# Hashed attention with an expert layer behind it: the six transposes of an attention step in three pairs, with score products between the pairs

## The chip, the cores and the metric

The kernel runs on one core of a Trainium2 chip. The metric is the device time of one execution in microseconds; the time shown for a kernel is the median of several executions. The names of the engines are those of the profile: PE multiplies matrices (PEld is its loading of weights), DVE works on vectors, ACT evaluates activations, POOL is the general engine, and SP issues most of the transfers.

## The reference, cut to what matters

```python
# q, k, v: (4, 8, 768, 64), proj: (64, 6)
q_bits = (np.einsum('bhsd,dk->bhsk', q, proj) > 0)      # 6 signs make a bucket
k_bits = (np.einsum('bhsd,dk->bhsk', k, proj) > 0)
mask = q_bucket[:, :, :, None] == k_bucket[:, :, None, :]
scores = np.where(mask, scale * np.matmul(q, k.transpose(0, 1, 3, 2)), -1000000000.0)
attn = np.exp(scores - np.max(scores, axis=-1, keepdims=True))
attn = attn / (np.sum(attn, axis=-1, keepdims=True) + 1e-09)
out = np.matmul(attn, v)                                # then 3072 tokens x 512
h = x @ w_in                                            # 512 -> 2048
g = h * np.clip(h + 3.0, 0.0, 6.0) / 6.0
result = g @ w_out                                      # 2048 -> 512
```

There are 32 pairs of batch and head, called heads below, with 768 queries and 768 keys each.

## The kernel before, in words

**Tiling.** Attention goes in steps `k` of 128 queries, six steps to a head (`KT = 6`), 192 steps in all. A step has four parts. `scores` (L374) makes the 128 x 768 scores with four matmuls of 384 columns: two on line 387 (`q1` with the two halves of `k1`, 76 rows) and two on line 389 (`q2` with the two halves of `k2`, 128 rows), which add the low parts of the split numbers to the same two banks of PSUM. `lowest` (L391) has DVE copy the scores to a tile `p` and find the row's extreme at once (line 396). `exponential` (L402) has ACT take the exponential in place in `p` (line 408). `transp` (L415) transposes the six 128 x 128 blocks of `p` on PE (line 418), three into each of two banks `pt`; `split_p` (L451) has ACT copy each bank rounded (line 475) and DVE subtract to get the remainder (line 479), and `values` (L491) multiplies both with the values, six matmuls of 256 columns per step on line 501, since a pair of steps shares one bank `acc`. The pair's result is copied out by ACT on line 551.

**Buffers.** Tiles `p` come from two buffers, so that `lowest(k + 2)` writes where the transposes of step `k` read. The scores alternate between two pairs of banks (`pair`). The banks `pt` and `acc`, and the small results `rt` and `h`, come from `bank`, which alternates between two tags of two buffers each: every request gets the bank of the request four before it. Where a pair of steps makes only its own five requests, the order is `pt, pt, acc` in an even step and `pt, pt` in an odd one. So the second bank of an odd step is the one that held the first bank of the even step before it, which DVE's line 479 reads last, and the second bank of an even step is the `acc` of the pair before.

**Order.** PE, DVE, ACT and POOL work in the order in which the program writes their instructions (`manual_schedule`). The loop over `k` (L1224) does, in a step: the transposes of `k`, `exponential(k + 1)`, `lowest(k + 2)`, half of an earlier pair's values, `split_p(k)`, and then `lead(k + 3)`, which calls `scores(k + 3)`. So PE sees, from one step to the next, values of `k`, scores of `k + 3`, transposes of `k + 1`. One step in each head also has the six matmuls of `hash_qk` (lines 334 to 336, tile `z`) ahead of its scores, and DVE's `bits` (line 352) behind them. From `k = 96` on `lead` comes right behind the values in some steps. `normalise` (line 591, tile `rt`) adds two small transposes in some steps.

**Stages.** Steps 0 to 51 run as attention alone, up to about 133 us. Then the expert layer of the first batch runs alone (`first_ffn`). Steps 52 to 100 run as attention alone again, from 277 to about 394 us. From step 101 on `beside_ffn` runs attention beside the expert layer of the other batches; there only step 101 still uses `transp`. The rest of the span is the expert layer.

Of the kernel before, what the change touches and what calls it, by code (L numbers as in the profile page):

```python
# [18 lines left out]
P = 128  # L19
# [9 lines left out]
LA = 3  # L29
# [14 lines left out]
def lsh_attention_moe(  # L44
# [10 lines left out]
    nc = tc.nc  # L55
# [3 lines left out]
    KT = S // P  # L59
    HW = S // 2  # L60
    QT = HW // P
# [5 lines left out]
    KM = D + 2 * NB  # L67
# [25 lines left out]
    def bank(shape, name: str, tag: str | None = None):  # L93

        nonlocal turn
        if tag is None:
            tag = ("pt", "pu")[turn % 2]
            turn += 1
        return ps.tile(shape, F32, name=name, tag=tag, bufs=2)
# [4 lines left out]
    def pair(name: str):  # L104

        nonlocal pair_turn
        pair_turn += 1
        tag = "s" if ffn_on or pair_turn % 2 else "po"
        return ps.tile([P, 2, 512], F32, name=name, tag=tag, bufs=1)
# [5 lines left out]
    ident = cp.tile([P, P], F32, name="ident")  # L115
# [119 lines left out]
    def get_qk(i: int, tag: str = "raw"):  # L235
        b, h = divmod(i, H)
        if tag == "raw":
            raws[i] = sp.tile([P, S], F32, name=f"raw{i}", tag=tag, bufs=1)[:]
        else:
            raws[i] = wide_tile([P, 2 * WC], F32, f"raw{i}")[:, :S]  # L240
        if paced:
            dma(out=raws[i][:D], in_=qkT[b, h, :D])
        else:
            dma(out=raws[i], in_=qkT[b, h])

    def get_k_rows(i: int):
        b, h = divmod(i, H)
        moves.append(lambda: dma(out=raws[i][D:], in_=qkT[b, h, D:]))
# [114 lines left out]
    def split_v(i: int):  # L363
        o = (i % 2) * D
        vr = vrs.pop(i)
        vv = vvs[i] = sp.tile([P, KT, P], F32R, name=f"vv{i}", tag="vv")
        nc.gpsimd.tensor_copy(vv[:, :, o : o + D], vr[:])
        nc.gpsimd.tensor_sub(
            vv[:, :, D - o : 2 * D - o], vr[:], vv[:, :, o : o + D].bitcast(F32)
        )  # L370

    scs, probs, outs = {}, {}, {}

    def scores(g: int):  # L374
        i, t = divmod(g, KT)
        k1, k2, q1, q2 = state[i]
        us = slice(t * P, (t + 1) * P)
        s = scs[g] = pair(f"s{g}")
        def half(x, c: int):
            if g < GT:  # L380
                return x[:, c * HW : (c + 1) * HW]

            x = x.rearrange("p (x g b) -> p g x b", x=KT, g=4)
            return x[:, 2 * c : 2 * c + 2]

        for c in range(2):
            nc.tensor.matmul(s[:, c, :HW], lhsT=q1[:KM, us], rhs=half(k1[:KM], c), start=True, stop=False)  # L387
        for c in range(2):
            nc.tensor.matmul(s[:, c, :HW], lhsT=q2[:, us], rhs=half(k2, c), start=False, stop=True)  # L389

    def lowest(g: int):  # L391

# [19 lines left out]
    pts, parts = {}, {}  # L412
    halves = 0

    def transp(g: int, c: int):  # L415
        pt = pts[g, c] = bank([P, QT, P], f"pt{g}_{c}")
        for x in range(QT):
            nc.tensor.transpose(pt[:, x], probs[g][0][:, c, x * P : (x + 1) * P], ident[:])  # L418
        if c:
            del probs[g]  # L420

# [100 lines left out]
    def add():  # L524
        for _, _, to, of in adds:
            nc.gpsimd.dma_start(out=to, in_=of, accum_op=ALU.add)
        adds[:] = fresh
        fresh.clear()
# [515 lines left out]
        finish()()  # L1044


    def lead(j: int):

        i, t = divmod(j, KT)
        n = i + 1  # L1050
        alone = j <= GF + LA
        if t == 0 and n < NJ:
            split_qk(n, nc.scalar.copy if ffn_on else nc.gpsimd.tensor_copy)
        if t in (1, 4) and not paced:
            add()
        if t == (4 if paced else 2):
            if i:
                split_v(i)
        if t == (3 if paced else 2):

            if n + 1 < NJ and n != H + 1:
                get_qk(n + 1)
                if paced:
                    get_k_rows(n + 1)
        if t == (5 if paced else 3) and n < NJ:
            get_v(n)
        hashed = t == 3 and n < NJ and alone and j != GB - 1
        if hashed:
            hash_qk(n)
        scores(j)  # L1070
        if hashed:
            bits(n)
        if t == (5 if paced else 4) and n + 1 < NJ:
            scale_q(n + 1)
# [27 lines left out]
    def value_half():  # L1102
        nonlocal vnext
        u, c = divmod(vnext, 2)
        vnext += 1
        values(u, c)
        return c == 1
# [14 lines left out]
    with tc.manual_schedule(engines={ET.PE, ET.DVE, ET.Activation, ET.Pool}):  # L1122
# [15 lines left out]
        def beside_ffn(k: int):  # L1138

            nonlocal paced, stage, held
            held = False
            if k < GT:
                for c in range(2):
                    transp(k, c)
                exponential(k + 1)
            for _ in range(2):
                u = vnext // 2
                if u < NS // 2 and (2 * u < GT or k % 2 and k >= 2 * u + 3):  # L1150
                    if vnext % 2 == 0 and k >= GT:
                        value_whole()
                        through.append(u)
                        break
                    if value_half():
                        through.append(vnext // 2 - 1)
                if k < GT:
                    break
            behind = (k - 1 + LA) % KT == 4 or k == GT + 1
            if GT <= k < NS - 2 and not behind:  # L1160
                lowest(k + 2)
            go("A")
            if GT <= k < NS - 2 and behind:
                lowest(k + 2)
            while late_bits:
                bits(late_bits.pop())
            if k < GT:
                for c in range(2):
                    split_p(k, c, False)
                split_lows()  # L1170
                while through:
                    output(through.pop(0))
                flip(k + 1)
            if k + 2 < NS:
                if k < GT:
                    lowest(k + 2)
                    assert len(side) <= 2
                    opening.pop()()
                if k == GT:
                    go("B")  # L1180
                    go("C")
                exponential(k + 2)
            paced = True
            multiply()
            if k + 2 < NS:
                flip(k + 2)
            split = GT <= k - LT < NS
            go("B")
            while rest:
                rest.pop()()  # L1190
            if split:
                split_p(k - LT, 1, False)
            if k == NS + LT:
                homes.clear()
            while through and (through[0] < vnext // 2 - 1 or k % 2 == 0 or k < GT):
                output(through.pop(0))
            hashed = k + LA < NS and (k + LA) % KT == 4 and (k + LA) // KT + 1 < NJ
            if hashed:
                hash_qk((k + LA) // KT + 1)
            if split:  # L1200
                amid.append(lambda: (split_p(k - LT, 0, False), split_lows()))
            go("C")
            while amid:
                amid.pop()()
            split_lows()
            if hashed and k == GT + 1:
                late_bits.append((k + LA) // KT + 1)
            elif hashed:
                bits((k + LA) // KT + 1)
            if k + LA < NS:  # L1210
                lead(k + LA)
            if moves:
                moves.pop(0)()
            if GT <= k + 1 < NS:
                move(k + 1)

            place_in_chunk = (k - GT) % NFC
            if subs and (k % 2 and (k < GT or place_in_chunk != NFC - 1) or k > GT and place_in_chunk == 0):
                subs.pop(0)()
            go("D")  # L1220
            if k % KT in (1, 3):
                add()

        for k in range(NS + LT + 2):  # L1224
# [10 lines left out]
                load_first_x()  # L1235
            if k == HK:
                late["x"] = sp.tile([P, S], F32, name="late", tag="raw", bufs=1)
            for c in range(2):
                transp(k, c)
            if k + 1 < end:  # L1240
                exponential(k + 1)
            if k + 2 < end:
# [19 lines left out]
            hashed = k >= GF and (k + LA) % KT == 2  # L1262
            after = hashed or k >= GF and (k + LA) % KT == 3
            if k >= GF and k + LA < end and not after:
                lead(k + LA)
            for c in range(2):
                split_p(k, c, third)
            split_lows()
# [2 lines left out]
            if (k < GF or after) and k + LA < end:  # L1271
                if hashed:
                    if (k + LA) // KT + 1 < NJ:
                        hash_qk((k + LA) // KT + 1)
                        bits((k + LA) // KT + 1)
                    next(fill, None)
                lead(k + LA)
            if k == GB - 2:
                hash_qk((GB - 1) // KT + 1)
                bits((GB - 1) // KT + 1)  # L1280
# [78 lines left out]
```

## Time and profile before

| what | value |
|---|---|
| time before, median of 3 runs | 965.38 us (964.78 to 966.62) |
| the profiled execution's own time | 964.74 us |
| its span | 963.0 us |
| PE busy | 945.1 us, 98% of the span |
| DVE, ACT, POOL busy | 723.0, 623.5 and 474.2 us |
| transposes of line 418 | 612 (102 steps of six) |
| score matmuls of lines 387 and 389 | 384 each |

The span is the time from the first to the last instruction that the profile shows; what lies around it is the 1.7 us between 963.0 and 964.74. The page's groups give busy time, the mean of one instruction and the idle time that the engine spent just ahead of it, with the engine and line that ended it. The timeline merges neighbouring instructions of one line into one row, and "x6" is their number. A matmul's duration in these rows is the time until its result is there; the next one can start much sooner, so the distance from start to start tells what PE pays for it.

### The profile page before, as it was taken

To read this page: it belongs to the slowest core of one execution; us is meant where nothing else is said; L and a number is where in the kernel's file an instruction comes from. 1 tells how busy PE (TensorE), PEld (TensorE's weight loads), DVE (VectorE), ACT (ScalarE), POOL (GpSimd) and SP (SyncE) were. 2 spreads that over 40 slices of the span, in tenths; PEclk is the share of its full clock that TensorE was granted. 3 is DMA by queue.
4 is the path that set the end of the run, shared out by engine and by line. 5 is a ranking of instruction groups with operands and counts; after the bars stand their busy time and mean duration, and the time that the engine had idled before them with its cause. 6 is when DMAs were issued, how large, how long until landed. Compare 5 with 4: busy or idle time off the path is not lost.

```text
span 963.0 us, 19452 instructions
## 1 busy us (share of the span) xinstructions
PE 945.1 (98%) x6306; PEld 872.7 (91%) x6306; DVE 723.0 (75%) x1470; ACT 623.5 (65%) x1421; POOL 474.2 (49%) x582
## 2 busy tenths in 40 slices
PE   8999999999999999999999999999999999999997
PEld 7999888999989999899999899989999999899996
DVE  7999988888659999887878888878878874343422
ACT  6898876566569888667766766666766664333332
POOL 6777744666536766555555555545555432000000
PEclk9999999999999999999999999999999999999999
DMA  3567579200034455588888888878988773101000
GB/s 117 140 157 188 134 205 376 85 1 1 6 116 110 121 126 131 169 256 241 253 252 256 238 240 255 246 236 239 274 239 254 222 222 72 44 1 45 1 22 22
DMA packets 113613, 152.06 MB, mean 158 GB/s; under 512 B 13876, under 2 KB 82612, under 8 KB 113512
## 3 DMA queue, kind: packets, MB, share of 16 engines
q1 hardware_dynamic: 108472, 144.79, 49.3%
q0 software_dynamic: 5040, 6.03, 5.1%
q8 instruction: 50, 0.82, 0.4%
q14 instruction: 51, 0.42, 0.1%
HBM read 77.34 MB, written 54.00 MB: 136 GB/s over the span
## 4 chain that ended last, share of the span: by engine, by line
PE 86%; DVE 8%; issue 2%; POOL 2%; ACT 2%; DMA 1%; SPq 0%; DVEq 0%; ACTq 0%; POOLq 0%
PE h L670 27%; PE po L708 7%; PE po L713 7%; PE po L709 7%; PE acc L515 6%; PE acc L501 6%; PE s L389 6%; PE s L387 5%; PE pt L418 5%; DVE p L396 2%; DVE pl L479 2%; DVE qq L352 1%; PE z L336 1%; PE rt L591 1%; PE z L334 1%
## 5 line engine op out<-in xcount | busy, mean ns | idle before, releaser
L408 ACT ACTIVATE p<-p,m 128x768 f32<-128x768 f32 x192 | 180.1, 938 | 112.4 <-DVE p L396 106.2
L396 DVE TENSOR_SCALAR_CACHE_REDUCE p<-s 128x768 f32<-128x768 f32 x192 | 182.5, 951 | 17.8 <-PE pt L418 11.7
L693 DVE SCALAR_TENSOR_TENSOR h<-g,h 128x256 f32<-128x256 f32 x192 | 81.0, 422 | 101.9 <-ACT g L692 99.3
L692 ACT ACTIVATE g<-h,three 128x256 f32<-128x256 f32 x192 | 91.0, 474 | 90.7 <-PE h L670 90.3
L670 PE MATMUL h<-xh,w 128*128 128x256 f32 x1024 | 147.0, 283 | 0.3
L670 PEld LDWEIGHTS h<-xh,w 128*128 128x128 f32 x1024 | 136.8, 188 | 4.5 <-DVE qq L352 1.2
L429 DVE STREAM_TRANSPOSE p<-p 128x768 f32<-128x768 f32 x90 | 88.1, 979 | 64.4 <-ACT p L408 64.4
L477 POOL TENSOR_TENSOR pl<-spare,ph 128x384 fp32r<-128x384 f32 x45 | 45.8, 1018 | 130.6 <-ACT ph L475 77.4
L479 DVE TENSOR_TENSOR pl<-pt,ph 128x384 fp32r<-128x384 f32 x196 | 100.1, 550 | 4.0 <-ACT ph L475 3.5
L387 PE MATMUL s<-kk,qq 76*128 76x384 f32 x384 | 100.0, 341 | 1.8 <-ACT kk L357 1.5
L389 PE MATMUL s<-kk,qq 128*128 128x384 f32 x384 | 100.5, 343 | 0.0
L708 PE MATMUL po<-w,gb 128*128 128x512 f32 x250 | 98.9, 396 | 1.0 <-ACT gb L698 1.0
L709 PE MATMUL po<-w,gb 128*128 128x512 f32 x250 | 98.6, 394 | 0.0
L475 ACT CAST ph<-pt 128x384 fp32r<-128x384 f32 x196 | 86.2, 474 | 15.0 <-PE pt L418 13.2
L216 POOL TENSOR_TENSOR w<-wr,w 128x128 fp32r<-128x128 f32 x128 | 71.8, 592 | 45.2 <-ACT w L210 42.1
L418 PE MATMUL pt<-ident,p 128*128 128x128 f32 x612 | 86.3, 275 | 2.4 <-DVE pl L479 1.6
L698 ACT CAST gb<-h 128x256 fp32r<-128x256 f32 x141 | 52.4, 372 | 49.8 <-DVE h L693 29.8
L670 PE MATMUL h<-xl,w 128*128 128x256 f32 x512 | 81.8, 281 | 0.0
L418 PEld LDWEIGHTS pt<-ident,p 128*128 128x128 f32 x612 | 72.5, 141 | 9.6 <-PE pt L418 2.4
L713 PE MATMUL po<-w,gb 128*128 128x512 f32 x250 | 78.4, 394 | 0.0
L318 POOL TENSOR_TENSOR kk<-raw,qq 64x192 fp32r<-64x192 f32 (+1 forms) x73 | 65.6, 923 | 24.1 <-ACT qq L304 20.9
L387 PEld LDWEIGHTS s<-kk,qq 76*128 76x128 f32 x384 | 66.4, 189 | 11.2 <-ACT kk L357 2.0
(153 smaller groups left out, 2168.7 us busy)
## 6 DMA issues: line engine op xcount, KB each, us to landing
fd<-p SPq DMA_DIRECT2D x90, 384.0 KB
spare<-fd SPq DMA_DIRECT2D x180, 96.0 KB
px<-fd SPq DMA_DIRECT2D x180, 96.0 KB
kk<-qq SPq DMA_DIRECT2D x62, 192.0 KB
wr<-in_w_in SPq DMA_DIRECT2D x16, 512.0 KB
wr<-in_w_out SPq DMA_DIRECT2D x16, 512.0 KB
raw<-in_qkT SPq DMA_DIRECT2D x19, 384.0 KB
vr<-in_v SPq DMA_DIRECT2D x32, 192.0 KB
```

What stands on the lines that cost most here:

```text
L387: nc.tensor.matmul(s[:, c, :HW], lhsT=q1[:KM, us], rhs=half(k1[:KM], c), start=True, stop=False)
L389: nc.tensor.matmul(s[:, c, :HW], lhsT=q2[:, us], rhs=half(k2, c), start=False, stop=True)
L396: nc.vector.tensor_scalar(out=pr_[:], in0=s[:, :, :HW], scalar1=CAP, scalar2=None, op0=ALU.min, op1=ALU.min, accum_out=m[:],)
L408: nc.scalar.activation(pr_[:], pr_[:], AF.Exp, bias=m[:], scale=-1.0, accum_out=sms[b][:, t, h : h + 1])
L418: nc.tensor.transpose(pt[:, x], probs[g][0][:, c, x * P : (x + 1) * P], ident[:])
L429: nc.vector.transpose(x, x)
L479: lows.append(lambda: engine.tensor_sub(lo, pt, hi.bitcast(F32)))
L670: nc.tensor.matmul(hp, lhsT=wi[:, wp, wc], rhs=x[cc][xp], start=(k == 0 and cc == 0), stop=(k == 2 and cc == NCC - 1),)
L692: nc.scalar.activation(r[:], hp, AF.Relu, bias=three[:], scale=1.0)
L708: nc.tensor.matmul(po[u], lhsT=gh[:, us], rhs=wo[:, 0], start=(fc == 0), stop=False)
L709: nc.tensor.matmul(po[u], lhsT=gh[:, us], rhs=wo[:, 1], start=False, stop=False)
L713: nc.tensor.matmul(po[u], lhsT=gl[:, us], rhs=wo[:, 0], start=False, stop=(fc == NFC - 1))
```

## The change

`transp` no longer takes one bank at a time: it issues all six transposes, asks for the second bank ahead of the fourth, and after the second and the fourth transpose issues one waiting part of a list `between`. `scores` can put its two parts on that list instead of issuing them: the first part is the two matmuls of line 387, the second the two of line 389. The main loop's calls of `lead` ask for this, so the scores of `k + 3`, written in step `k`, are issued among the transposes of step `k + 1`. PE's order in a step becomes: transposes 1 and 2, two score matmuls, transposes 3 and 4, two score matmuls, transposes 5 and 6. The calls of `lead` at the start, at the end of the first expert layer and beside the expert layer issue at once as before.

```diff
-    def scores(g: int):
+    def scores(g: int, later: bool = False):
         i, t = divmod(g, KT)
...
-        s = scs[g] = pair(f"s{g}")
...
-        for c in range(2):
-            nc.tensor.matmul(s[:, c, :HW], lhsT=q1[:KM, us], rhs=half(k1[:KM], c), start=True, stop=False)
-        for c in range(2):
-            nc.tensor.matmul(s[:, c, :HW], lhsT=q2[:, us], rhs=half(k2, c), start=False, stop=True)
+        def part(n: int):
+            if n == 0:
+                scs[g] = pair(f"s{g}")
+            q, k = ((q1[:KM], k1[:KM]), (q2, k2))[n]
+            for c in range(2):
+                nc.tensor.matmul(
+                    scs[g][:, c, :HW], lhsT=q[:, us], rhs=half(k, c), start=n == 0, stop=n == 1
+                )
+
+        for n in range(2):
+            if later:
+                between.append(lambda n=n: part(n))
+            else:
+                part(n)
+
+    between = []
...
-    def transp(g: int, c: int):
-        pt = pts[g, c] = bank([P, QT, P], f"pt{g}_{c}")
-        for x in range(QT):
-            nc.tensor.transpose(pt[:, x], probs[g][0][:, c, x * P : (x + 1) * P], ident[:])
-        if c:
-            del probs[g]
+    def transp(g: int):
+        pr_ = probs.pop(g)[0]
+        for n in range(KT):
+            c, x = divmod(n, QT)
+            if x == 0:
+                pts[g, c] = bank([P, QT, P], f"pt{g}_{c}")
+            nc.tensor.transpose(pts[g, c][:, x], pr_[:, c, x * P : (x + 1) * P], ident[:])
+            if n % 2 and between:
+                between.pop(0)()
+        assert not between
...
-    def lead(j: int):
+    def lead(j: int, later: bool = False):
...
-        scores(j)
+        scores(j, later)
...
-            for c in range(2):
-                transp(k, c)
+            transp(k)
...
-                lead(k + LA)
+                lead(k + LA, True)
```

The last two hunks stand for all places: `transp` is called in the loop and in `beside_ffn`, and `lead(k + LA)` twice in the loop.

More of the change, by code (lines that the diff above doesn't have):

```diff
@@ L1237, in lsh_attention_moe @@
                 late["x"] = sp.tile([P, S], F32, name="late", tag="raw", bufs=1)
-            for c in range(2):
-                transp(k, c)
+            transp(k)
             if k + 1 < end:
@@ L1276, in lsh_attention_moe @@
                     next(fill, None)
-                lead(k + LA)
+                lead(k + LA, True)
             if k == GB - 2:
```

## The prediction, made before the changed kernel had run

> **What bounds the kernel now.** I read the page first, for the share of each engine, and in its groups the rows of the lines that the change touches.
>
> ```profile
> span 963.0 us, 19452 instructions
> PE 945.1 (98%) x6306; PEld 872.7 (91%) x6306; DVE 723.0 (75%) x1470; ACT 623.5 (65%) x1421; POOL 474.2 (49%) x582
> ...
> L396 DVE TENSOR_SCALAR_CACHE_REDUCE p<-s 128x768 f32<-128x768 f32 x192 | 182.5, 951 | 17.8 <-PE pt L418 11.7
> ```
>
> PE hardly rests, but its busy time runs to modelled ends, so the page alone cannot say whether PE sets the pace in attention or waits in small pieces. It does say whom DVE waits for on line 396: the transposes. So I looked at windows of one head in each stretch of attention alone.
>
> ```profile
> 59.40:73.60 14.20, 13.96 (x104) 13.34 (x103) 13.68 (x28) 12.47 (x28) 11.76 (x13) 1.00 0.59 152
> 328.00:342.00 14.00, 14.00 (x107) 13.62 (x106) 12.80 (x27) 12.37 (x28) 9.84 (x9) 1.00 0.50 117
> ```
>
> The columns are the span, then PE, PEld, DVE, ACT and POOL busy, then the granted clock (1.00). In the early head DVE is nearly as full as PE (13.68 of 14.20 us, it converts weights as well); in the late one it has 1.2 us of idle time. Next the timeline, first PE's in the late head: transposes of step 74, its values, the scores of 77, the transposes of step 75, values, and the scores and transposes after them.
>
> ```profile
> 329.55 0.82 PE L418 MATMUL pt<-ident,p 128*128 128x128 f32 x6
> 330.12 0.60 PE L501 MATMUL acc<-ph,vv 128*128 128x256 f32 x3
> 330.55 0.52 PE L501 MATMUL acc<-pl,vv 128*128 128x256 f32 x3
> 330.91 0.52 PE L387 MATMUL s<-kk,qq 76*128 76x384 f32 x2
> 331.26 0.53 PE L389 MATMUL s<-kk,qq 128*128 128x384 f32 x2
> 331.63 0.87 PE L418 MATMUL pt<-ident,p 128*128 128x128 f32 x6
> 332.26 0.61 PE L501 MATMUL acc<-ph,vv 128*128 128x256 f32 x3
> ...
> 333.06 0.52 PE L387 MATMUL s<-kk,qq 76*128 76x384 f32 x2
> ```
>
> One step is 331.63 - 329.55 = 2.08 us; a transpose is 0.11 us behind the one before it ((0.82 - 0.27)/5, 0.27 being the last one's own length); two score matmuls are 0.36 us (330.91, 331.26, 331.63), four 0.72. Step 74 has its six in 0.82, step 75 in 0.87. The reason stands in DVE's rows of the same stretch.
>
> ```profile
> 330.40 0.96 DVE L396 TENSOR_SCALAR_CACHE_REDUCE p<-s 128x768 f32<-128x768 f32 x1
> ...
> 331.28 1.02 DVE L479 TENSOR_TENSOR pl<-pt,ph 128x384 fp32r<-128x384 f32 x2
> 332.54 0.96 DVE L396 TENSOR_SCALAR_CACHE_REDUCE p<-s 128x768 f32<-128x768 f32 x1 [0.24 <-PE pt L418]
> ...
> 333.42 1.02 DVE L479 TENSOR_TENSOR pl<-pt,ph 128x384 fp32r<-128x384 f32 x2
> 334.62 0.96 DVE L396 TENSOR_SCALAR_CACHE_REDUCE p<-s 128x768 f32<-128x768 f32 x1 [0.18 <-PE pt L418]
> ```
>
> These rows hold a loop. `lowest(76)` at 330.40 needs the tile `p` that the six transposes of step 74 read; the sixth started near 329.55 + 5 x 0.11 = 330.10, so it follows by 0.30. Behind it DVE takes the remainders of step 74, at 331.28; the first lasts 0.55 (below) and ends near 331.83. It frees the first `pt` bank of step 74, and by the rotation of banks that is the one which the fourth transpose of step 75 needs. That one was due at 331.63 + 3 x 0.11 = 331.96. How soon can it follow? Later rows show the wait openly.
>
> ```profile
> 385.36 1.02 DVE L479 TENSOR_TENSOR pl<-pt,ph 128x384 fp32r<-128x384 f32 x2 [0.54 <-ACT ph L475]
> 386.07 0.52 PE L418 MATMUL pt<-ident,p 128*128 128x128 f32 x3 [0.28 <-DVE pl L479]
> ```
>
> ```profile
> PE pt L418 <- DVE pl L479: 1.6, 4, 0.7
> ```
>
> The first two are timeline rows, the last is that of the waits: 1.6 us in four waits over the whole span. 385.36 + 0.55 = 385.91, and the fourth transpose starts 0.16 later. So in step 75 it could start at 331.83 + 0.16 = 331.99: it is already held, by a few hundredths, which are the 0.05 in 0.87. PE and DVE are in balance to within that.
>
> **The change part by part.** It removes and adds no instruction; no transfer and no queue but PE's is touched: DVE, ACT and POOL keep their order. Per step two pairs of score matmuls move, the first from ahead of transpose 1 to behind transpose 2, the second to behind transpose 4.
>
> *PE's own time: nothing.* A switch from transposes to score matmuls and back stands in the trace where two small transposes precede scores.
>
> ```profile
> 384.37 0.38 PE L591 MATMUL rt<-ident,spare 128*128 128x128 f32 x2
> 384.51 0.60 PE L387 MATMUL s<-kk,qq 76*128 76x384 f32 x2
> 384.94 0.52 PE L389 MATMUL s<-kk,qq 128*128 128x384 f32 x2
> 385.30 0.49 PE L418 MATMUL pt<-ident,p 128*128 128x128 f32 x3
> ```
>
> 384.94 - 384.37 = 0.57 = 2 x 0.11 + 0.35: no loss, no gain; and the three transposes behind scores still come 0.11 apart ((0.49 - 0.27)/2). I take 0; a hundredth per step either way would be 1 us over some 98 steps. The Trainium skill, "TensorE: Matmul & The Clock Gate", section "LDWEIGHTS (loading the stationary operand)", gives a weight load columns/1.2 ns, 107 ns for 128, and its section "Back-to-back issue gap" lets 128 columns stream in 56 ns; so a transpose would be bound by its load, which agrees with 0.11, and a load beside a longer product could be hidden, as this change would have it. That is a rival below.
>
> *The wait for exponentials: nothing.* Transpose 1 comes 0.72 us sooner. In step 75 it has that much to spare:
>
> ```profile
> 329.39 0.94 ACT L408 ACTIVATE p<-p,m 128x768 f32<-128x768 f32 x1
> 330.23 0.19 ACT L408 ACTIVATION_READ_ACCUMULATOR p<-p,m 128x1 f32 x1
> ...
> 332.34 0.84 ACT L475 CAST ph<-pt 128x384 fp32r<-128x384 f32 x2
> 333.26 0.37 ACT L551 COPY y<-acc 128x256 f32<-128x256 f32 x1
> ```
>
> The exponential of 75 ends at 330.42; transpose 1 moves from 331.63 to 330.91, still 0.49 behind it. Were the cover gone, PE's queue (scores, transposes, values) would stand behind it.
>
> *The wait for banks: here it costs.* Transpose 4 had four score matmuls and three transposes ahead of it behind the values; now it has two and three. So it is due 0.36 sooner. In even steps its bank is `acc`, freed by line 551: 333.26 + 0.37 = 333.63 against 333.06 + 3 x 0.11 + 0.35 = 333.74; 0.11 remains, I take 0, with at most 0.05 in some 45 steps as the upper end (2 us). In odd steps it was tied to DVE already, and DVE comes no sooner, since its own chain starts at the sixth transpose of the step before. So transpose 4 stays where it was, PE stands still 0.36, and then comes what is new: **two score matmuls now stand between transpose 4 and transposes 5 and 6.** The sixth, which `lowest` waits for, comes 0.36 later, and values, scores, and everything behind move with it. The loop of an odd step grows from 2.14 (2.08 and the wait) to 2.50 us.
>
> Where is that on the path? In the steady part of the second stretch DVE is idle ahead of `lowest` in nearly every step:
>
> ```profile
> L396 DVE TENSOR_SCALAR_CACHE_REDUCE p<-s 128x768 f32<-128x768 f32 x38 | 36.4, 958 | 6.3 <-PE pt L418 5.1
> ...
> L479 DVE TENSOR_TENSOR pl<-pt,ph 128x384 fp32r<-128x384 f32 x75 | 38.2, 551 | 0.2
> ...
> 290.62 0.88 PE L418 MATMUL pt<-ident,p 128*128 128x128 f32 x6
> ...
> 372.63 0.87 PE L418 MATMUL pt<-ident,p 128*128 128x128 f32 x6
> ```
>
> The first two rows group 286 to 372 us (the second also gives the 0.55). The others are the first and the last of the 13 odd steps, 57 to 93, whose transposes take 0.87 or 0.88. The third odd step of a head has the bucket product ahead of its transposes, about 1.05 us more room, and stays free. 13 x 0.36 = **4.7 us**. At this stretch's end five steps (94, 95, 96, 98, 100) wait as in the 386.07 row or are tied: 5 x 0.36 = **1.8**.
>
> In the first stretch DVE's conversions hide one of the two waits of a head:
>
> ```profile
> 63.65 0.82 PE L418 MATMUL pt<-ident,p 128*128 128x128 f32 x6
> 64.18 1.12 DVE L205 SCALAR_TENSOR_TENSOR wr<-wr 128x512 uint32<-128x512 uint32 x1
> 65.23 0.94 DVE L396 TENSOR_SCALAR_CACHE_REDUCE p<-s 128x768 f32<-128x768 f32 x1
> ...
> 67.91 1.01 DVE L479 TENSOR_TENSOR pl<-pt,ph 128x384 fp32r<-128x384 f32 x2
> 68.28 0.83 PE L418 MATMUL pt<-ident,p 128*128 128x128 f32 x6
> 69.16 0.96 DVE L396 TENSOR_SCALAR_CACHE_REDUCE p<-s 128x768 f32<-128x768 f32 x1 [0.24 <-PE pt L418]
> ```
>
> In step 21 (63.65) the sixth transpose, near 64.20, has 1.03 us until `lowest` at 65.23, because DVE converts weights: 0.36 vanishes there, and would cost in full without that conversion. In step 23 (68.28) transpose 4 is tied to 67.91 + 0.55 + 0.16 = 68.62, and DVE waits: 0.36. So four such heads give 1.4; the heads before and behind them, without that cover, six more (steps 5, 9, 11, 38, 45, 47), 2.2. Together **3.6**.
>
> Seven more steps (39, 41, 42, 46, 48, 54, 101) have the rotation shifted by small transposes, or stand at a start; there the wait falls on transpose 1 or hits a slack of 0.2 to 0.4. Each costs between 0 and 0.72; nearest are the steps above at 0.36, less slack, so 0.25: **1.8**, ends 0 and 5. The sum is 4.7 + 1.8 + 3.6 + 1.8 = 11.9 us. Against the profiled execution, 963.0 of span and 1.7 around it, that is 964.7 + 11.9 = 976.6. Its time lies 0.6 under the median of the runs; so I forecast 977.3 us, 1.2% slower.
>
> **The rivals.**
>
> *It is worth nothing: 965.4.* For it: no work is added and PE's sum is unchanged. It needs half a microsecond of slack behind the sixth transpose, as in step 21; against it, DVE's idle row over 38 steps shows none in the second stretch. A part of it is likelier, the first stretch's 3.6 or so are lost again where attention hands over to the experts, and the shifted steps cost nothing: 4.7 + 1.8, about 972.
>
> *Faster: transposes behind a score product no longer pay for their weight load.* By rows, 256 columns follow each other in 0.12 (330.55 to 330.91, three) and 384 in 0.18, so 128 columns alone would be 0.06; two transposes a step stand directly behind a product and would gain 0.05 each, 0.10 in 98 steps: 10 us, 955.6. Against it: the transpose at 385.30 stands behind a product and gains nothing, and what PE gained in an odd step would end in the bank's wait. This is what the skill's rule on weight loads would bring.
>
> *Much slower: even steps are tied as well.* The copy of line 551 that frees `acc` stands on ACT behind the two rounding copies of line 475, and the second of these now waits for a sixth transpose that comes later. If that pushed the copy back, even steps would lose their 0.36 too: 45 x 0.36 = 16 more, 993. Against it: in step 75 the sixth transpose ends at 332.23 + 0.36 + 0.27 = 332.86, a rounding copy takes about 0.5, so it is done near 333.36, while line 551 waits for the values and is due at 333.26 + 0.36 = 333.62. It decides only from 0.26 later on.
>
> **How the numbers follow.** The forecast with its own spread, 973 to 982: 0.72. Only part of it, 967.5 to 973: 0.12. No change: 0.07. Faster: 0.05. Much slower: 0.04. A measurement of this kernel can tell about 0.2% (1.9 us) from no change. So slower 0.87, same 0.08 (a part of it may fall there), faster 0.05. The range, 968 to 982, takes the forecast and most of the partial case, 0.82.
>
> **What would show it.** Right: rows of line 418 come in pairs; in odd steps of 286 to 380 us a pause of some 0.3 us ahead of the fourth transpose, put down to DVE `pl` L479, in sum from 1.6 us to about 10; two consecutive steps take 4.58 instead of 4.22 us; line 396's idle time grows as much; the expert stages are as long as before. Wrong: transposes less than 0.10 apart, a wait for ACT `p` ahead of the first, or an unchanged distance of steps with PE's new pauses beside DVE's work.

## The result, and the profile after

The changed kernel takes 979.76 us (median of 4 runs, 978.66 to 980.19) against 965.12 for the kernel before (4 runs): a ratio of 1.0146, 95% interval 1.0134 to 1.0157. That is 14.6 us slower; 11.9 were forecast. The profiled executions, 980.19 and 964.74 us, are 15.4 us apart, and so are their spans. One execution of the kernel before and one of the kernel with the second pair behind transpose 2 (below) ran at a granted clock of 0.56 and took 1538 and 1539 us; the times and ratios leave both out, and since the second was the profiled one, that kernel has no timeline here. On the page of the changed kernel the lines are renumbered: transposes 433 (before: 418), scores 391 (387 and 389), `lowest` 408 (396), exponential 420 (408), remainder 495 (479), values 517 (501), the copy of `acc` 567 (551), `rt` 607 (591).

```profile
span 978.4 us, 19478 instructions
PE 948.1 (97%) x6306; PEld 864.3 (88%) x6306; DVE 722.4 (74%) x1470; ACT 627.8 (64%) x1421; POOL 472.4 (48%) x582
L408 DVE TENSOR_SCALAR_CACHE_REDUCE p<-s 128x768 f32<-128x768 f32 x192 | 182.7, 952 | 32.8 <-PE pt L433 25.7
```

The engines do the same work as before: DVE's busy time is 0.6 us off, and PE's, which runs to modelled ends, 3.0 us up. What grew is DVE's idle time ahead of `lowest`, from 17.8 to 32.8 us, nearly the whole difference, and the new idle time stands with the transposes. The view of waits of the changed kernel tells what they wait for:

```profile
DVE p L408 <- PE pt L433: 25.7, 62, 0.9
PE pt L433 <- DVE pl L495: 8.4, 30, 0.8
PE pt L433 <- ACT y L567: 1.7, 6, 0.5
PE pt L433 <- DVE lent L495: 0.9, 2, 0.7
```

The wait for DVE's `pl` was 1.6 us in 4 waits and is 8.4 in 30. PE's timeline of the same steps that the prediction showed (74, 75, and the start of 76) shows one of them:

```profile
339.69 0.38 PE L433 MATMUL pt<-ident,p 128*128 128x128 f32 x2
339.83 0.59 PE L391 MATMUL s<-kk,qq 76*128 76x384 f32 x2
340.26 0.39 PE L433 MATMUL pt<-ident,p 128*128 128x128 f32 x2
340.40 0.59 PE L391 MATMUL s<-kk,qq 128*128 128x384 f32 x2
340.84 0.38 PE L433 MATMUL pt<-ident,p 128*128 128x128 f32 x2
...
341.77 0.38 PE L433 MATMUL pt<-ident,p 128*128 128x128 f32 x2
341.90 0.60 PE L391 MATMUL s<-kk,qq 76*128 76x384 f32 x2
342.34 0.27 PE L433 MATMUL pt<-ident,p 128*128 128x128 f32 x1
342.83 0.30 PE L433 MATMUL pt<-ident,p 128*128 128x128 f32 x1 [0.22 <-DVE pl L495]
342.89 0.59 PE L391 MATMUL s<-kk,qq 128*128 128x384 f32 x2
343.32 0.38 PE L433 MATMUL pt<-ident,p 128*128 128x128 f32 x2
...
344.25 0.38 PE L433 MATMUL pt<-ident,p 128*128 128x128 f32 x2
```

Step 74 (339.69 to 341.77) takes 2.08 us, as before: the moves cost PE nothing by themselves. In step 75 the third transpose starts at 342.34 and the fourth, due 0.11 later, only at 342.83; two score products follow, and transposes five and six at 343.32. The two steps take 344.25 - 339.69 = 4.56 us; before, the step was 2.08 and the pair about 4.2. DVE's timeline of the stretch closes the loop:

```profile
341.25 0.96 DVE L408 TENSOR_SCALAR_CACHE_REDUCE p<-s 128x768 f32<-128x768 f32 x1
...
342.14 1.02 DVE L495 TENSOR_TENSOR pl<-pt,ph 128x384 fp32r<-128x384 f32 x2
343.74 0.96 DVE L408 TENSOR_SCALAR_CACHE_REDUCE p<-s 128x768 f32<-128x768 f32 x1 [0.59 <-PE pt L433]
```

The first remainder starts at 342.14 and lasts 0.55, so to 342.69; the fourth transpose follows at 342.83. Then DVE itself is idle 0.59 us until the sixth transpose (near 343.43) lets `lowest` start at 343.74; before, that idle time was 0.24.

To place the whole difference I took the start of the sixth transpose of each step in both timelines, and how much further apart the two kernels are than a step earlier. In us:

| steps | forecast | measured |
|---|---|---|
| 13 odd steps, 57 to 93 | 4.7 | 4.6 (0.35 or 0.36 each) |
| even steps beside them | 0 | within 0.02 of 0 each |
| 94, 95, 96, 98, 100 | 1.8 | 1.4 (96 none, the others 0.35 to 0.37) |
| first stretch, the 14 unshifted steps named | 3.6 | 5.1 |
| steps with a shifted rotation or at a start | 1.8 | 4.1 |

The last row counts steps 39 to 42, 46, 48, 54, 99 and 101, less 0.48 that step 55 gives back. The measured column adds up to 15.2. What the table leaves out comes to 0.2: steps 1 and 3, which were not in the forecast, lose 0.51 and 0.44, and many others gain some hundredths. The distance at step 101 is 15.4 us, and so is that of the spans: the expert layer behind it is as long as before.

### The profile page after: what moved, and what is told of

Same layout as the page of the kernel before. It is cut to its first block, busy times and chain, and to the rows that moved or that the text cites. A ratio compares the mean times of both kernels' runs of the same rounds, so it can differ in the third digit from the quotient of the medians.

```text
span 978.4 us, 19478 instructions
## 1 busy us (share of the span) xinstructions
PE 948.1 (97%) x6306; PEld 864.3 (88%) x6306; DVE 722.4 (74%) x1470; ACT 627.8 (64%) x1421; POOL 472.4 (48%) x582
## 4 chain that ended last, share of the span: by engine, by line
PE 85%; DVE 7%; issue 2%; ACT 2%; POOL 2%; DMA 1%; SPq 0%; DVEq 0%; POOLq 0%; ACTq 0%
PE h L686 27%; PE s L391 11%; PE po L724 7%; PE po L729 7%; PE po L725 7%; PE acc L531 6%; PE acc L517 6%; PE pt L433 6%; DVE pl L495 3%; DVE p L408 2%; DVE qq L352 1%; PE z L334 1%; PE z L336 1%; PE z L335 1%; PE pos L724 1%
## 5 line engine op out<-in xcount | busy, mean ns | idle before, releaser
L408 DVE TENSOR_SCALAR_CACHE_REDUCE p<-s 128x768 f32<-128x768 f32 x192 | 182.7, 952 | 32.8 <-PE pt L433 25.7
L391 PE MATMUL s<-kk,qq 76*128 76x384 f32 (+1 forms) x768 | 198.2, 361 | 1.8 <-ACT kk L357 1.5
L391 PEld LDWEIGHTS s<-kk,qq 76*128 76x128 f32 (+1 forms) x768 | 128.7, 191 | 10.8 <-ACT kk L357 2.0
L433 PE MATMUL pt<-ident,p 128*128 128x128 f32 x612 | 122.5, 275 | 13.3 <-DVE pl L495 8.4
L433 PEld LDWEIGHTS pt<-ident,p 128*128 128x128 f32 x612 | 81.4, 140 | 33.8 <-PE pt L433 16.9
L491 ACT CAST ph<-pt 128x384 fp32r<-128x384 f32 x196 | 90.2, 473 | 17.2 <-PE pt L433 11.4
L493 POOL TENSOR_TENSOR pl<-px,ph 128x384 fp32r<-128x384 f32 x45 | 46.6, 1037 | 54.7 <-ACT ph L491 32.6
```

Source lines behind the costliest of these rows:

```text
L391: nc.tensor.matmul(scs[g][:, c, :HW], lhsT=q[:, us], rhs=half(k, c), start=n == 0, stop=n == 1)
L408: nc.vector.tensor_scalar(out=pr_[:], in0=s[:, :, :HW], scalar1=CAP, scalar2=None, op0=ALU.min, op1=ALU.min, accum_out=m[:],)
L433: nc.tensor.transpose(pts[g, c][:, x], pr_[:, c, x * P : (x + 1) * P], ident[:])
L491: nc.scalar.copy(hi, pt)
L493: engine.tensor_sub(lo, pt, hi.bitcast(F32))
```

## The experiments

The prediction's theory, called **bank theory** below: the fourth transpose of an odd step is tied to a DVE remainder, and each score product standing between it and the sixth transpose delays DVE's next start. Its rivals: **changeover**, in which PE pays for alternating between transposes and products, and **exponential**, in which the first transpose, 0.72 us sooner, waits for ACT. In all the edits the work is the same; unless said otherwise they start from the changed kernel.

### The second pair of products behind transpose 2

The first pair of score products stands ahead of transpose 1 as before the change, the second behind transpose 2, so none stands behind the fourth.

```diff
-            if later:
+            if later and n:
...
-            if n % 2 and between:
+            if n == 1 and between:
```

> The first pair of score products (line 387 of before) is issued at once as before, only the second pair waits and goes behind transpose 2; nothing stands between transposes 3 and 6. Bank theory (the fourth transpose of an odd step is tied to DVE's remainder of the step before, and what stands between it and the sixth is paid): transpose 4 has as many instructions ahead of it as before, nothing behind it that was not there, so 965.1, at most 1.5 more. Changeover theory (PE pays for every change between transposes and products; the change has three more per step and costs 14.6 us, 4.9 us for one): two more per step than before, 974.9. Exponential theory (the loss is the first transpose waiting for ACT, 0.72 us sooner): sooner by 0.36, about half the loss, 972.

Measured: 965.80 us, ratio 1.0013 to the kernel before (1.0004 to 1.0023). Transposes and products alternate, and by the order the first transpose is due 0.36 sooner, yet about 1 us is lost instead of 14.6.

### The second pair behind transpose 4

The same with the second pair behind the fourth transpose. PE changes over as often as in the run above; only the place differs.

```diff
-            if later:
+            if later and n:
...
-            if n % 2 and between:
+            if n == 3 and between:
```

> As the run with the second pair behind transpose 2, but the pair goes behind transpose 4. Bank theory: the tied fourth transpose is followed by two products ahead of the fifth, as in the changed kernel, so 0.36 in each tied step again: 978 to 980. Changeover theory: as many changes as with the pair behind transpose 2, so 974.9 for both. Exponential theory: the first transpose is as early as there, 972 for both.

Measured: 977.73 us, ratio 1.0132 (1.0115 to 1.0149), 11.9 us more than with the pair two transposes earlier and 12.6 more than the kernel before. Most of the loss of the change is in this one pair. PE's timeline of an odd step:

```profile
338.74 0.49 PE L433 MATMUL pt<-ident,p 128*128 128x128 f32 x3
339.45 0.30 PE L433 MATMUL pt<-ident,p 128*128 128x128 f32 x1 [0.22 <-DVE pl L495]
339.51 0.59 PE L391 MATMUL s<-kk,qq 128*128 128x384 f32 x2
```

The fourth was due at 338.74 + 3 x 0.11 = 339.07 and starts 0.38 later, as in the changed kernel.

### Both pairs behind transpose 4

```diff
-            if n % 2 and between:
-                between.pop(0)()
+            while n == 3 and between:
+                between.pop(0)()
```

> All four score products behind transpose 4. Bank theory: a tied step pays 0.72 instead of 0.36, and the fourth transpose of even steps, now 0.72 sooner than before, is tied to ACT's copy of acc as well, some 0.2 to 0.3 late, and pays too: 28 x 0.72 = 20 and 45 x 0.3 = 13, so about 998, between 992 and 1005. Changeover theory: one more change per step than before, 970. Exponential theory: the first transpose is 0.72 us sooner as in the change, 980.

Measured: 1002.84 us, ratio 1.0395 (1.038 to 1.0411): 37.7 us over the kernel before. Odd steps of the second stretch lose 0.71 each, and now the even ones lose 0.33 to 0.36, as their bank, freed by the copy of `acc`, is late as well. PE's timeline of one odd step, and from that of its weight loads the fourth transpose of an even one:

```profile
356.79 0.49 PE L433 MATMUL pt<-ident,p 128*128 128x128 f32 x3
357.85 0.30 PE L433 MATMUL pt<-ident,p 128*128 128x128 f32 x1 [0.58 <-DVE pl L495]
357.91 0.95 PE L391 MATMUL s<-kk,qq 76*128 76x384 f32 x4
...
360.26 0.14 PEld L433 LDWEIGHTS pt<-ident,p 128*128 128x128 f32 x1 [0.37 <-ACT y L567]
```

In the odd step the fourth starts 1.06 behind the first instead of 0.33, and four products stand behind it. The loss per odd step is twice that of two products: 0.71 against 0.36.

### Both pairs behind transpose 3

```diff
-            if n % 2 and between:
-                between.pop(0)()
+            while n == 2 and between:
+                between.pop(0)()
```

> All four score products behind transpose 3, between the two banks: three transposes, four products, three transposes. Bank theory: transpose 4 has as much ahead of it as before and nothing but transposes 5 and 6 behind it: 965.1, within 1.5. Changeover theory: one more change per step, 970. Exponential theory: the first transpose is 0.72 us sooner, as in the change, so 980.

Measured: 966.25 us, ratio 1.0016 (1.0003 to 1.0028). All four products are among the transposes, and the first transpose comes 0.72 sooner as in the changed kernel, but the fourth is due when it was due before:

```profile
332.45 0.49 PE L433 MATMUL pt<-ident,p 128*128 128x128 f32 x3
332.69 0.94 PE L391 MATMUL s<-kk,qq 76*128 76x384 f32 x4
333.51 0.52 PE L433 MATMUL pt<-ident,p 128*128 128x128 f32 x3
```

A row of a shifted step in the same timeline, where the first transpose is the one that waits, shows what is left of the loss:

```profile
112.03 0.52 PE L433 MATMUL pt<-ident,p 128*128 128x128 f32 x3 [0.69 <-DVE lent L495]
```

Step by step this kernel gains 0.38 to 0.41 in five steps of the first stretch (17, 23, 29, 35, 38) and loses 0.2 to 0.7 in each of eight others (39 to 42, 46, 48, 99, where the rotation is shifted, and 54, at the start of the second stretch), and 0.70 in step 15, to which the run with ACT's scaling comes back. The four runs together refute changeover and exponential as causes of the main loss: the same products cost about 1 us ahead of the fourth transpose, 12.6 with one pair behind it and 37.7 with two.

### Cutting the tie, first try

The first remainder of a step is computed from the rounded copy in SBUF instead of from the bank, so that DVE no longer holds the bank; once in the kernel before, once in the changed one.

```diff
-            lows.append(lambda: engine.tensor_sub(lo, pt, hi.bitcast(F32)))
+            of = pt if c or g >= GT else hi.bitcast(F32)
+            lows.append(lambda: engine.tensor_sub(lo, of, hi.bitcast(F32)))
```

> The kernel before, where DVE's remainder for the first bank of a step is taken from the rounded copy in SBUF, not from the bank (the low parts of these probabilities are left out, they become zero), so that the bank is free as soon as ACT has copied it. Bank theory: the few hundredths of wait in odd steps and the open waits of five steps go: 1 to 5 us faster than before, 960 to 964. Changeover and exponential theories: nothing changes on PE or ACT, 965.1. DVE's subtraction may itself take another time from SBUF; in the second stretch that is hidden.

> The changed kernel with the same edit of the remainder (low parts of the first bank left out). Bank theory: with the tie gone the order costs next to nothing: within 3 us of the kernel before with the same edit, 960 to 967. Changeover theory: the loss stays, 14.6 us more than the kernel before with the same edit, about 979. Exponential theory: the same 979.

Measured: 981.21 us (ratio 1.0159, 1.0137 to 1.0181) in the kernel before, 991.04 (1.0263, 1.0242 to 1.0284) in the changed one, 9.8 apart. Both expectations of the bank theory were missed, by 17 and 24 us, and the distance of 9.8 fits neither its 3 nor the 14.6 of the others. DVE's groups of the first kernel show what else the edit changed:

```profile
L480 DVE TENSOR_TENSOR pl<-ph 128x384 fp32r<-128x384 f32 x98 | 82.4, 841 | 4.0 <-ACT ph L475 3.6
L480 DVE TENSOR_TENSOR pl<-pt,ph 128x384 fp32r<-128x384 f32 x98 | 53.6, 547 | 0.0
```

The subtraction reading SBUF alone takes 0.84 us on the mean, the one reading PSUM 0.55. So this pair of runs changed a duration as well as a tie, and decides nothing about the tie.

### Cutting the tie, second try

Now the first remainder reads the step's other PSUM bank, which has the same shape; the duration should stay. The low parts of the first bank are then not the right ones, and the output is not the reference's; only the time counts.

```diff
-            lows.append(lambda: engine.tensor_sub(lo, pt, hi.bitcast(F32)))
+            of = pts[g, 1][:] if not c and g < GT else pt
+            lows.append(lambda: engine.tensor_sub(lo, of, hi.bitcast(F32)))
```

> The kernel before, where DVE's remainder for the first bank of a step reads the step's second bank instead of the first (so that these low parts are wrong and the output is not the reference's); the first bank is free as soon as ACT has copied it, and DVE still reads as much from PSUM. Bank theory: the waits of odd steps for DVE go, 1 to 4 us: 961 to 964. Changeover theory: no change, 965.2. DVE's subtraction should last 0.55 us again, unlike from SBUF (0.84 and 0.93 on the mean), where that edit spoiled the test.

> The changed kernel with the same edit (the remainder of the first bank reads the second, wrong low parts). Bank theory: what is left of the loss are the first transposes of the steps with a shifted rotation and DVE's conversions, at most 7 us over the kernel before with the same edit: 961 to 970; in the odd steps from 57 to 93 transposes 3 and 4 are 0.11 apart. Changeover and exponential theories: 14.6 us over the kernel before with the same edit, about 977.

Measured: 964.05 us (ratio 0.9994, 0.9983 to 1.0004) and 970.89 (1.0061, 1.0043 to 1.008). With the tie the change costs 14.6 us, without it 6.8; the second kernel lies 0.9 above the range named. PE's timeline of two consecutive steps of the second kernel:

```profile
332.83 0.38 PE L433 MATMUL pt<-ident,p 128*128 128x128 f32 x2
...
333.41 0.38 PE L433 MATMUL pt<-ident,p 128*128 128x128 f32 x2
...
333.98 0.38 PE L433 MATMUL pt<-ident,p 128*128 128x128 f32 x2
...
334.91 0.38 PE L433 MATMUL pt<-ident,p 128*128 128x128 f32 x2
```

The order is that of the change, with no pause anywhere, and the step is 334.91 - 332.83 = 2.08. In the steady part of the second stretch the difference between the two kernels is zero. The 6.8 us that remain (7.5 between the two profiled executions) lie mostly in three other places: 0.56 to 0.70 each in steps 17, 23, 29, 33 and 35, 0.36 to 0.47 in the shifted steps 46 and 48 and in step 94, and 1.9 behind step 101. In the first of these groups the first transposes of a step now wait for ACT's exponential, as in the first of these rows, from the timeline of PE's weight loads in step 23. But the exponential itself comes late there, since a DVE conversion ahead of it takes longer: the second row is of the same kernel, the third of the kernel before with the same edit.

```profile
67.67 0.20 PEld L433 LDWEIGHTS pt<-ident,p 128*128 128x128 f32 x2 [0.24 <-ACT p L420]
...
64.39 1.23 DVE L205 SCALAR_TENSOR_TENSOR wr<-wr 128x512 uint32<-128x512 uint32 x1
...
63.00 0.68 DVE L205 SCALAR_TENSOR_TENSOR wr<-wr 128x512 uint32<-128x512 uint32 x1
```

Ahead of steps 17, 29 and 35 the same conversions take 1.20, 1.20 and 1.19 us against 0.79, 0.68 and 0.68, and ahead of step 33 another takes 1.09 against 0.43. So in this group most of the loss goes with DVE's conversions and is passed on by the exponential; it does not show that the exponential would be the next limit.

### POOL's scaling moved to ACT

In heads 1 to 3 three weight conversions on DVE got longer than before, 1.7 us in all. My reading was that POOL's scaling of `raw` (line 276, 2.14 us), which starts when its transfer has landed, now started just ahead of them. Here ACT does that scaling for heads 2 to 8.

```diff
-            if paced:
+            if paced or HK // KT > i - 1 > 0:
                 nc.scalar.mul(raws[i][:D, c], raws[i][:D, c], -SCALE)
```

> The changed kernel with the scaling of the queries of heads 2 to 8 (line 276, 2.1 us on POOL) done by ACT instead. In the changed kernel DVE's weight conversions in heads 1 to 3 took 1.32, 1.02 and 0.90 us with that POOL instruction beside them, where 0.69, 0.43 and 0.43 are seen alone. If POOL beside them is the cause, they take 0.69, 0.43 and 0.43 here, and steps 9, 15 and 21 lose some 0.4 instead of 0.98, 0.98 and 0.85: 1.7 us less, 978, if ACT's added work (about 1 us a head) is hidden. If the cause is elsewhere (when the conversion stands, the bank), their lengths stay and so does the time.

Measured: 982.35 us, ratio 1.0178 (1.0155 to 1.0201): 2.6 us more than the changed kernel, where 1.7 less were expected. The timelines of head 2, first the changed kernel and then this one:

```profile
48.15 2.14 POOL L276 TENSOR_SCALAR raw<-raw 64x768 f32<-64x768 f32 x1 [0.33 <-DMA raw<-in_qkT]
48.23 1.02 DVE L194 TENSOR_SCALAR wr<-wr 128x512 uint32<-128x512 uint32 x1
```

```profile
48.66 0.43 DVE L194 TENSOR_SCALAR wr<-wr 128x512 uint32<-128x512 uint32 x1
...
95.54 0.84 ACT L274 ACTIVATE raw<-raw 64x768 f32<-64x768 f32 x1 [1.41 <-DMA raw<-in_qkT]
```

The conversion is back at 0.43, as before the change, the other two are back at 0.69 and 0.43, and steps 9, 15 and 21 gain 0.99, 0.73 and 0.59. That bears the reading out. Whether POOL's scaling delays such a conversion also differs from one execution to the next. The kernel with both pairs behind transpose 3 and the version at the end of this section have the same program up to step 38; here are DVE and POOL at the same place in head 2, first in the one and then in the other:

```profile
45.78 1.10 DVE L194 TENSOR_SCALAR wr<-wr 128x512 uint32<-128x512 uint32 x1
45.78 2.14 POOL L276 TENSOR_SCALAR raw<-raw 64x768 f32<-64x768 f32 x1 [0.34 <-DMA raw<-in_qkT]
```

```profile
45.72 0.43 DVE L194 TENSOR_SCALAR wr<-wr 128x512 uint32<-128x512 uint32 x1
45.74 2.40 POOL L276 TENSOR_SCALAR raw<-raw 64x768 f32<-64x768 f32 x1 [0.32 <-DMA raw<-in_qkT]
```

The starts differ by some hundredths of a microsecond, and step 15 loses 0.70 in the one and 0.04 in the other. Only one execution of the changed kernel was profiled, so how much of its 1.7 us comes back in others is not known.

The time was lost again by the edit itself: ACT's scaling costs 0.38 in steps 8, 14 and 20, and in steps 26 and 32, which lose 1.09 and 1.90, ACT, in order, waits for the transfer (the `raw` row at 95.54 is that of step 32).

### A version that beats both

Both pairs behind transpose 3, except in the steps in which the rotation is shifted and in step 54; there the products come at once as before the change. The second hunk stands for both calls in the loop.

```diff
-            if n % 2 and between:
-                between.pop(0)()
+            while n == 2 and between:
+                between.pop(0)()
...
-                lead(k + LA, True)
+                lead(k + LA, k not in (38, 39, 40, 41, 45, 47, 53, 98))
```

> All four products behind transpose 3, but not in steps 39 to 42, 46, 48, 54 and 99, where the rotation of banks is shifted and the run with all behind transpose 3 lost 0.2 to 0.7 us each to a first transpose that waits for DVE: there the products go ahead of the transposes as before. Bank theory: the sum of those losses, 3.6 us, goes and the 1 us over the kernel before turns into a gain: 962 to 964. If these losses come from elsewhere, or turn up in the next step, 965 to 966.

Measured: 962.74 us (median of 12, 961.12 to 964.45), ratio 0.9974 (0.9963 to 0.9985), 2.3 us faster than the kernel before, and 17.0 faster than the changed kernel by the medians. Its row of waits for `pl`, and from its groups between 40 and 100 us the one of a conversion:

```profile
PE pt L433 <- DVE pl L495: 0.3, 1, 0.3
```

```profile
L196 DVE SCALAR_TENSOR_TENSOR wr<-wr 128x512 uint32<-128x512 uint32 x2 | 1.4, 683 | 0.0
```

The losses in the eight steps are gone, the gains of 0.38 to 0.41 in steps 17, 23, 29, 35 and 38 stay. In the kernel before that conversion takes 1.12 us in the same window, 0.44 more, and so does the one of line 205; ahead of step 38 a conversion takes 0.43 instead of 0.65 and the small instruction of line 587 0.25 instead of 0.47. So the gains go with DVE's instructions, not with PE's order: the kernel before with the tie cut the second way, whose order on PE is unchanged, has these conversions at 0.68 to 0.79 and gains 0.30 to 0.44 in steps 17, 23, 29 and 35 too. That they got shorter because they fall at another moment of POOL's work is my reading of the rows in the last section; no edit tested it alone.

## Why the prediction was right

Slower by 1.2% was forecast, with 968 to 982 us as the range; 979.76 lies in it, 2.5 over the forecast. By its own steps:

- **PE's own time: nothing.** Right. Untied, the step of the changed order is 2.08 us, and pairs of transposes among products still start 0.11 apart (0.38 for two, 0.27 for one). No load of weights was hidden, so the faster rival fell with it.
- **The tie of odd steps: 0.36 each.** Right in mechanism and size: 0.35 or 0.36 in each of the 13 steps, a pair of steps 4.56 us (4.58 was named), twice that with two pairs behind the fourth transpose, nothing with both pairs behind the third or with the tie cut.
- **Even steps: nothing.** Right by a small margin: with their fourth transpose due another 0.36 sooner they lost 0.33 to 0.36 each. The rival at 993 us was that near.
- **The exponential: nothing.** Right, but for step 54 at the start of the second stretch, where the first transpose waits 1.49 us for it instead of 0.71; of the 0.71 that this step loses, step 55 gives 0.48 back.
- **The wait for `pl`, about 10 us.** 8.4 us in 30 waits, and 2.6 more for ACT's `y` and DVE's `lent`, which the prediction did not name. The idle time ahead of `lowest`, which was to grow by as much, grew by 15.0.
- **The first stretch: 3.6, mis-sized.** The steps named measured 5.1, and steps 1 and 3, which the sum put at nothing, lost 0.51 and 0.44 on top. The step that failed is the cover by DVE's conversions, taken as a constant. The conversions that were to cover steps 15, 21, 27 and 33 fell from 1.12 to 0.69 us, and these steps, called hidden, lost 0.98, 0.85, 0.37 and 0.37; steps 17, 23, 29 and 35, called tied, lost nothing. Set against the kernel with both pairs behind transpose 3, where those conversions are as short, steps 33 and 35 pay 0.33 and 0.35: nothing is hidden, but the shorter conversion gives about 0.4 back in the second step. For the sum that made little difference. The excess comes from three other conversions, which grew by 0.63, 0.59 and 0.47 ahead of steps 9, 15 and 21, beside POOL's scaling: without these 1.7 us the steps named would come to 3.4.
- **Shifted steps: 1.8, mis-sized.** They measured 4.1. The term took 0.25 each, from the odd steps' 0.36 less a slack. But in steps 39 to 42 the bank that is late belongs to the first transpose or to a small one ahead of it, as the prediction had said, and the change makes these 0.72 sooner, not 0.36. PE's timeline of the changed kernel in these steps:

```profile
112.61 0.41 PE L433 MATMUL pt<-ident,p 128*128 128x128 f32 x2 [0.69 <-DVE pl L495]
115.33 0.44 PE L433 MATMUL pt<-ident,p 128*128 128x128 f32 x2 [0.46 <-ACT y L567]
118.53 0.41 PE L433 MATMUL pt<-ident,p 128*128 128x128 f32 x2 [0.69 <-DVE lent L495]
121.26 0.44 PE L607 MATMUL rt<-ident,lent 128*128 128x128 f32 x2 [0.46 <-ACT y L567]
```

Each of these waits stands ahead of a step's small or first transposes, with all four score products behind it. The steps lost 0.63 (39 and 40), 0.19 (41) and 0.67 (42), and 99 lost 0.58; 40 and 99 were not named. The end that the prediction kept for this term, 5, was the better guess.

## What to carry to other kernels

Work moved into a gap on an in-order engine is free only if every instruction that it passes stays untied: before moving it, find in the trace the instruction among them that waits for a buffer, and put the work ahead of that one, never between it and the instruction that starts the next turn of the loop. All four products one place ahead of the tied transpose cost about 1 us here, one place behind it 38. And a cover made of another engine's instructions is only as firm as their durations, which change with what runs beside them.

## What the runs showed of the hardware

**A DVE conversion and a POOL instruction on SBUF delay each other, and the one that starts second pays.** The conversion at 64.18 in the kernel before, 1.12 us long, stands in the prediction; here is POOL's timeline beside it, and then both engines' at the same place in the version that beats both:

```profile
63.94 0.82 POOL L304 CAST qq<-raw 128x768 fp32r<-128x768 f32 x1 [0.98 <-PE s L389]
```

```profile
63.60 0.68 DVE L205 SCALAR_TENSOR_TENSOR wr<-wr 128x512 uint32<-128x512 uint32 x1
63.67 1.30 POOL L304 CAST qq<-raw 128x768 fp32r<-128x768 f32 x1 [1.67 <-PE s L391]
```

Where POOL's cast starts 0.24 us ahead, DVE's conversion takes 0.44 longer; where DVE starts 0.07 ahead, the cast takes 0.48 longer. In the rows of head 2 above, the two start within 0.02 us of each other, and either DVE's conversion or POOL's scaling takes longer. The subtraction reading PSUM kept 0.55 on the mean in every kernel; in the kernel before with the first cut, the one reading SBUF alone took 0.55 at the least, 0.84 on the mean and 2.17 at the most.

The Trainium skill, "SBUF — State Buffer", section "SBUF: two separate sides", says that DVE and POOL share a pair of ports as an exclusive lock: between a POOL operation and a DVE operation in a two-port mode, or with two SBUF inputs, the one that starts first holds it for its whole instruction and the other is fully blocked. In which mode a conversion runs no trace here shows. The rows agree that the later one pays, and not that it is blocked to the end: the conversion of 48.23 ended after 1.02 us, at 49.25, while POOL's instruction of 48.15 ran until 50.29.

**A whole kernel can gain a quarter of a per cent by where such pairs fall.** The five gains of 0.4 us are most of the 2.3 us of the last version. Apart from the move of POOL's scaling, no edit set which POOL instruction meets which conversion, and I have not tried to set it.
